# A new stored order, with an accumulating form of the layernorm statistics, in an RWKV attention and Fourier mixing kernel

## The chip, the cores and the metric

The kernel runs on one core of one Trainium2 chip. The metric is the time of one execution on the device, in microseconds (us), the median of several runs. A core has five instruction queues that work side by side: PE (the matrix unit), ACT, DVE, POOL and SP. SP does no arithmetic here; it issues DMA transfers. Each queue takes its instructions strictly in order, and they wait for each other by semaphores.

## The reference

Two stages, for a batch of 4, 8 heads, 768 steps, head size 48. The first is a linear attention with a state of 48 x 48 per head:

```python
for t in range(S):
    cur = np.einsum('bhd,bhe->bhde', u[None] * kt, vt)
    y[:, :, t] = np.einsum('bhd,bhde->bhe', rt, state + cur)
    state = wt[:, :, :, None] * state + np.einsum('bhd,bhe->bhde', kt, vt)
```

Its output, with the heads side by side, is a row of 384 numbers for each of the 768 steps. The second stage mixes these rows:

```python
X = np.fft.fft(np.fft.fft(x, axis=1), axis=2)
u = x + np.real(X)
un = (u - mean(u)) / sqrt(var(u) + 1e-06)          # over the 384
out = u + np.maximum(un @ w_ch1, 0.0) @ w_ch2      # 384 -> 1536 -> 384
```

All inputs and the output are float32.

## The kernel before, in words

**Tiling.** Each batch is cut into 6 chunks of 128 steps, 24 in all; I write (b,c) for chunk c of batch b. A chunk is loaded as four tiles of 128 x 384 (r, k, v, w; L622, issued by SP). Per chunk, `attention` does this:

- ACT takes the logarithm of w (into `lb`), and PE sums it over the steps with triangular masks (L795 for one direction, L818 for the other; the sum can instead be formed by a subtraction on DVE, L832, form "sum_add" against "sum_two").
- ACT takes exponentials of the sums (L822, L848), and DVE or POOL form the decayed rows `rkh` = r·e and k·e (L849, and k·e in a call that the profile shows at L576), the product r·k (L800, shown at L576), r·k·u, its sum `dc` over each head (DVE, L863) and v·dc (`vtd`).
- `rkh` is transposed to `rkt`: by PE with an eviction by DVE or ACT (forms "tr_two", L890, and "tr_one", L902) or, in batch 3, by a DMA that SP issues (form "tr_dma", L880).
- PE forms the 128 x 128 products of a chunk for all heads (`amat`, L913), DVE masks them (L923; or ACT copies them and DVE or POOL masks the copy), PE updates the state (L950) and forms the chunk's output (L975, L978), to which v·dc is added on DVE (L989), or on PE by a float32 matmul with the identity (form "add_pe", L998).

After the 6 chunks of a batch, `mix` does the second stage for 6 blocks of 128 rows. The Fourier transform over steps is a product with cosine and sine tables of the folded rows (`sd`, `xf`; L1054), the one over the 384 is another (L1098) whose result is added to x into `uf`. Then come the statistics of each row: in batch 0 by an addition that also sums (L1115) and a Square on ACT that sums; in batches 1 to 3 by a plain addition (L1128), a `bn_stats` (L1155) and a `bn_aggr` (L1157) on DVE. The row without its mean (`un`) is transposed for three blocks at a time (one half of a batch: by PE, L1173, or by a DMA, L1180), multiplied with W1 (L1205), passed through ReLU into `ht` (ACT L1213 or DVE L1211), multiplied with W2 (L1224), scaled and added to `uf` (L1233) and stored (L1244). The weights come by POOL's DMA queue (L765, L770).

**Order.** The program is first recorded as a list of operations, each with its engines, buffers and a cost. Where an operation can be done in several forms, `choose` records all of them as alternatives. Which alternative is taken, which engine does an operation, and in which order each engine works, stands in the literal `ORDER`: five lists of operation numbers, one per queue, found offline by a planner in the class `_Prog`. `schedule` walks the lists and puts a planned time on every operation; its constants (costs in ns, `xfer` for the length of a transfer, `T_LAT` for the latency of a DMA transpose, `DMA_SW` for a software queue) serve this plan alone. `emit` writes the instructions in the order of the lists, with semaphores derived from buffers. So the lists set the order, and numbers in the lists are positions in the record: every alternative that is added renumbers what stands behind it.

`vec` is the helper that records an operation for DVE or POOL, `evict` one for ACT or DVE:

```python
def vec(n, fn, **kw):
    return op(None, {"pool": p_1(n), "dve": v_1(n)}, fn, port=("dve",), **kw)
```

Thirty-two small matmuls without use (L1291) and 16 at the start (L1257) stand in PE's list to keep its clock up; they are the same in number before and after.

## Time and profile before

| what | value |
|---|---|
| runs shown | 182.51, 183.09, 184.56 us; median 183.09 us |
| the profiled execution: its own time | 181.76 us |
| its span in the trace (first to last instruction) | 179.6 us |
| granted PE clock | 0.999 |
| instructions | 4554 |
| busy: ACT | 127.5 us (71%) |
| busy: POOL | 107.7 us (60%) |
| DMA | 29.28 MB, mean 163 GB/s |

The profile of one execution has a page (busy time by engine, the span in 40 slices with a digit of tenths for each, the chain of work that ended last, and groups of instructions by line) and a trace that can be asked for the same things over shorter stretches. A row of the timeline reads: start in us, length in us, engine, line, operation, output <- inputs with partitions x elements and type, count, and in brackets the idle time before it with what ended it. A row of groups reads: line, engine, operation, output <- inputs, count | busy us, mean ns of one | idle us before, and what ended it. The chain's rows read: start, length, engine, output, line. On one engine instructions are pipelined: one can start before the row of the one before has ended, so the cost of an instruction in a full queue is the distance between two starts.

### The profile page before, as it was taken

Reading aid. Unit: us, or ns where it says so; the run is one execution under the profiler, and the core shown is the slowest. Engines: PE = TensorE matmul, PEld = TensorE weight load, DVE = VectorE, ACT = ScalarE, POOL = GpSimd, SP = SyncE. Lnnn points to the kernel's source line nnn. Section 1 sums busy time; section 2 is a strip of 40 time slices with the busy share of each in tenths; the row PEclk is TensorE's granted clock in tenths of the full one; section 3 lists DMA queues with packets and bytes.
Section 4 is the critical chain, followed back from the end, with each engine's and each line's share of the span. In section 5 each row is a group of like instructions: output and inputs, shape, how many; then the busy total and the mean of one; then the engine's idle time right before and its main releaser. Section 6 shows DMA issues by size and latency. Waiting matters only on the chain.

```text
span 179.6 us, 4554 instructions
## 1 busy us (share of the span) xinstructions
PE 172.1 (96%) x1704; PEld 113.7 (63%) x1704; DVE 159.5 (89%) x378; ACT 127.5 (71%) x306; POOL 107.7 (60%) x134
## 2 busy tenths in 40 slices
PE   4989899999999999999999999999989999999994
PEld 2456556766666667777666666766656766655663
DVE  7899899989999899999999999999999997971643
ACT  2899978679996578799999897989960775062200
POOL 2557969496705888499999964997862140500000
PEclk9999999999999999999999999999999999999999
DMA  6999999999999689999997999989972213034033
GB/s 118 217 210 225 183 206 193 203 216 179 162 205 204 145 173 224 199 211 217 202 239 137 224 182 240 235 155 197 245 71 56 74 47 65 1 60 141 0 131 131
DMA packets 117302, 29.28 MB, mean 163 GB/s; under 512 B 112545, under 2 KB 117282, under 8 KB 117282
## 3 DMA queue, kind: packets, MB, share of 16 engines
q1 hardware_dynamic: 115698, 26.65, 72.3%
q0 software_dynamic: 1584, 2.36, 7.9%
q8 instruction: 13, 0.21, 0.5%
q14 instruction: 7, 0.06, 0.1%
HBM read 23.59 MB, written 4.72 MB: 158 GB/s over the span
## 4 chain that ended last, share of the span: by engine, by line
PE 72%; DVE 13%; ACT 7%; POOL 3%; DMA 3%; issue 1%; POOLq 0%; DVEq 0%; ACTq 0%
PE bank L1205 23%; PE bank L1224 23%; PE bank L1098 4%; PE bank L1054 3%; PE bank L913 3%; DMA rkt<-rkh 3%; PE bank L890 2%; PE bank L795 2%; PE bank L978 2%; DVE bst L1155 2%; PE bank L975 1%; DVE uf L1128 1%; ACT rkt L599 1%; PE bank L950 1%; PE bank L818 1%
## 5 line engine op out<-in xcount | busy, mean ns | idle before, releaser
L1224 PE MATMUL bank<-w,ht 128*128 128x384 bf16 (+2 forms) x300 | 53.1, 320 | 0.0
L1205 PE MATMUL bank<-unt,w 128*128 128x384 bf16 x288 | 52.9, 326 | 0.0
L1213 ACT ACTIVATE ht<-bank 128x384 bf16<-128x384 f32 x70 | 31.0, 496 | 21.1 <-PE bank L1205 20.9
L1224 PEld LDWEIGHTS bank<-w,ht 128*128 128x128 bf16 x300 | 27.8, 98 | 15.6
L1205 PEld LDWEIGHTS bank<-unt,w 128*128 128x128 bf16 x288 | 26.6, 98 | 15.8 <-ACT ht L1213 0.2
L923 DVE TENSOR_TENSOR ah<-bank,msk 128x512 bf16<-128x512 f32 x44 | 28.7, 682 | 0.8 <-PE bank L913 0.6
L576 POOL TENSOR_TENSOR rk<-in_r,in_k 128x384 f32<-128x384 f32 x22 | 21.8, 999 | 1.9 <-issue 1.4
L576 POOL TENSOR_TENSOR rkh<-in_k,e 128x384 bf16<-128x384 f32 x18 | 18.0, 1003 | 6.7 <-ACT e L836 4.9
L576 POOL TENSOR_TENSOR rk<-rk,ub 128x384 f32<-128x384 f32 x20 | 19.8, 998 | 3.3 <-DVE rk L576 2.1
L576 POOL TENSOR_TENSOR vtd<-in_v,dc 128x384 f32<-128x384 f32 x20 | 16.4, 829 | 5.1 <-DVE sd L576 1.8
L599 ACT ACTIVATE rkt<-bank 128x512 bf16<-128x512 bf16 (+1 forms) x23 | 16.3, 713 | 4.3 <-PE bank L902 2.8
L1233 DVE SCALAR_TENSOR_TENSOR osb<-bank,rstd,uf 128x384 f32<-128x384 f32 (+2 forms) x24 | 14.3, 594 | 5.5 <-PE bank L1224 3.5
L1211 DVE TENSOR_SCALAR ht<-bank 128x384 bf16<-128x384 f32 x26 | 13.5, 548 | 5.4 <-PE bank L1205 5.2
L863 DVE TENSOR_REDUCE dc<-rk 128x8 f32<-128x384 f32 x24 | 12.7, 544 | 0.4 <-POOL rk L576 0.4
L848 ACT ACTIVATE bank<-bank 128x384 f32<-128x384 f32 x22 | 10.6, 488 | 3.0 <-PE bank L795 2.7
L590 ACT ACTIVATE lb<-in_w 128x384 bf16<-128x384 f32 x24 | 12.6, 528 | 0.1
L590 ACT ACTIVATE un<-uf,agg 128x384 bf16<-128x384 f32 x19 | 11.2, 618 | 1.5 <-DVE agg L1157 0.9
L849 DVE TENSOR_TENSOR rkh<-bank,in_r 128x384 bf16<-128x384 f32 x22 | 11.9, 547 | 0.2 <-ACT bank L848 0.2
L590 ACT ACTIVATE vb<-in_v 128x384 bf16<-128x384 f32 x22 | 11.5, 530 | 0.4 <-DMA in_v<-in_v_dram 0.3
L822 ACT ACTIVATE e<-bank 128x392 f32<-128x392 f32 (+1 forms) x18 | 8.8, 498 | 3.9 <-PE bank L809 2.5
L978 PE MATMUL bank<-vb,ah 128*128 128x48 bf16 x192 | 11.2, 183 | 0.0
L576 POOL TENSOR_TENSOR xf<-sd 128x384 bf16<-128x384 f32 (+1 forms) x7 | 6.9, 1002 | 6.1 <-DVE xf L576 3.9
(178 smaller groups left out, 365.1 us busy)
## 6 DMA issues: line engine op xcount, KB each, us to landing
in_r<-in_r_dram SPq DMA_DIRECT2D x24, 192.0 KB, 3.9
in_k<-in_k_dram SPq DMA_DIRECT2D x24, 192.0 KB, 3.8
in_w<-in_w_dram SPq DMA_DIRECT2D x24, 192.0 KB, 3.8
in_v<-in_v_dram SPq DMA_DIRECT2D x24, 192.0 KB, 3.8
out_dram<-osb SPq DMA_DIRECT2D x23, 192.0 KB, 2.9
w<-in_moe_w_ch_dram POOLq DMA_DIRECT2D x2, 576.0 KB, 7.9
w<-in_moe_w_ch_dram POOLq DMA_DIRECT2D x1, 1152.0 KB, 10.7
out_dram<-osb SPq DMA_DIRECT2D x1, 128.0 KB, 1.8
```

The costliest lines, as they stand in the source:

```text
L576: return lambda e: e.tensor_tensor(out=o, in0=a, in1=b, op=f)
L590: return lambda e: e.activation(o, a, f, **kw)
L599: {"act": lambda e: e.activation(o(), i(), ACTF.Copy), "dve": lambda e: e.tensor_copy(out=o(), in_=i())}, **kw)
L849: op("dve", v_1(DM), lambda e: e.tensor_tensor(out=rh[:, :, 0:D], in0=ps(tce)[:, 0:DM].rearrange("t (h d) -> t h d", d=D), in1=rt[:, :, :] ...
L863: op("dve", v_1(DM), lambda e: e.tensor_reduce(out=dc[:, :], in_=rku[:, :, :], axis=mybir.AxisListType.X, op=ALU.add), r=[("RK", i2)], w=[ ...
L923: masked[n].append(op("dve", v_1(512), lambda e: e.tensor_tensor(out=ah[:, x:H:2, :], in0=ps(bk)[:, :].rearrange("p (h t) -> p h t", t=128 ...
L978: ins = e.matmul(ps(ty)[:, D * h:D * h + D], ah[:, h, :], vb[:, h, :], start=first and not ype, stop=True, skip_group_check=True)
L1205: ins = e.matmul(ps(t)[:, 0:384], W1[:, m, 256 * (j // 2) + j % 2:256 * (j // 2) + 256:2], unt[:, :, m, :], start=(m == 0), stop=(m == NM ...
L1211: {"dve": lambda e, j=j, t=t, ht=ht: e.tensor_scalar(out=ht[:, j, :], in0=ps(t)[:, 0:384], scalar1=su, scalar2=0.0, op0=ALU.mult, op1=ALU. ...
L1213: "act": lambda e, j=j, t=t, ht=ht: e.activation(ht[:, j, :], ps(t)[:, 0:384], ACTF.Relu, scale=su)},
L1224: ins = e.matmul(ps(t)[:, 0:hi - lo], ht[:, j, 128 * x:128 * x + 128], W2[:, j, lo:hi], start=(j == 0), stop=(j == NJ - 1))
L1233: op("dve", v_1(hi - lo) + 64, lambda e: e.scalar_tensor_tensor(out=o[:, lo:hi], in0=ps(t)[:, 0:hi - lo], scalar=rstd[:, kb:kb + 1], in1=u ...
```

## The change

Four things are changed.

1. `ORDER` is replaced. 1 operation less is on PE (559 to 558), 9 more on ACT (300 to 309), 3 fewer on DVE (372 to 369) and 3 fewer on POOL (130 to 127); SP has 133 in both. Read against the record, the new lists differ in these places above all:
   - *First loads:* before, SP issued r1, k1, w1, w0, u, r0, k0 first; after, w0, k1, u, r1, w1, k0, r0, w2 (the digit is the chunk of batch 0).
   - *Batch 0, products:* r·k of chunks (0,1), (0,2) and (0,3) and k·e of (0,0) go from POOL to DVE; r·k·u of (0,1), v·dc of (0,0) and k·e of (0,2) and (0,4) go from DVE to POOL.
   - *Batch 0, others:* chunk (0,1) takes its output addition on DVE (L989) instead of PE (L998; two other chunks keep that form); two casts of the transform in mix 0 go from DVE to ACT; evictions of transposes are dealt differently between ACT and DVE, with "tr_one" and "tr_two" swapped in six chunks. The decay sums of (1,0) take "sum_two" in place of "sum_add", those of (3,4) the reverse.
   - *Statistics:* blocks 0, 1 and 2 of mix 2 and block 2 of mix 3 take the new form `add_sum`.
   - *Late, on SP:* before, the order was: last loads of (3,5), load v of (3,4), outputs (1,5), (1,3), (1,4), DMA transposes of (3,5) and (3,4), transpose of the second half of mix 2. After, it is: load v of (3,4), transposes of (3,4) and (3,5), load v of (3,5), outputs (1,3), (1,5), transpose of the second half of mix 2, output (1,4). On PE, `amat` of these two chunks stands earlier by two groups of W2 matmuls and one state update. On POOL, k·e of (3,5) stands earlier.
2. Constants of the plan: a load counts 998 ns instead of 985, the stretch that a transfer of the software queue (the weights) takes up in the plan begins 200 ns earlier, the DMA transposes of (3,4) and (3,5) count 200 ns more and that of the second half of mix 2 200 ns more.
3. New buffers `MS` and `MCO`, with two small fills on DVE.
4. A new alternative `add_sum` for the statistics of batches 1 to 3. The bn_stats, bn_aggr and the operation that subtracts the mean are moved from behind the choice into each alternative.

The diff without the lists:

```diff
+    MS = [sb("ms%d" % i, [NC, 3], FP32) for i in range(2)]
+    MCO = sb("mco", [2], FP32)
...
                 a = max(sw_t, s + self.DMA_SW)
                 sw_t = a + o.xfer
+                a -= 200
...
-               w=[("in", n, i)], sem="in_%s%d" % (n, i), xfer=985)
+               w=[("in", n, i)], sem="in_%s%d" % (n, i), xfer=998)
...
+        op("dve", 40, fill(MCO[:, 0:1], 1.0 / DM), w=["MCO0"])
+        op("dve", 40, fill(MCO[:, 1:2], float(DM) ** -1.5), r=["MCO0"], w=["MCO"])
...
-               ... xfer=T_XFER, dma=(T_LAT[0], T_LAT[1] + 500))
+               ... xfer=T_XFER, dma=(T_LAT[0], T_LAT[1] + (700 if (b, c) >= (3, 4) else 500)))
...
+                def normed(mean, dep, kb=kb, un=un, iu=iu):
+                    op(None, {"act": a_sb(DM) + 95, "dve": v_2(DM) + 60},
+                       {"act": act(un, uf[:, kb, :], ACTF.Identity, scale=-1.0, bias=mean),
+                        "dve": ts(un, uf[:, kb, :], mean, -1.0, ALU.subtract, ALU.mult)}, port=("dve",),
+                       r=[("UF", i, kb), dep], w=[("UN", iu, kb % 3)])
+
+                def stats(kb=kb, bs=BST[n % 4], n=n):
+                    op("dve", v_1(DM), lambda e: e.bn_stats(bs[:, :], uf[:, kb, :]), ...)
+                    op("dve", 89, lambda e: e.bn_aggr(agg[:, kb, :], bs[:, :]), ...)
+                    normed(agg[:, kb, 0:1], ("AGG", i, kb))
...
+                def add_sum(kb=kb, t=t):
+                    whole()
+                    ms = MS[i]
+                    op("dve", v_1(DM) + 60, lambda e: e.scalar_tensor_tensor(
+                        out=uf[:, kb, :], in0=ps(t)[:, 0:DM], scalar=1.0, in1=xb[:, kb, 0:DM], op0=ALU.mult, op1=ALU.add,
+                        accum_out=ms[:, kb, 2:3]), r=[t, ("X", i, kb)], w=[("UF", i, kb), ("SUM", i, kb)])
+                    op("dve", 64, lambda e: e.tensor_tensor(
+                        out=ms[:, kb, 0:2], in0=ms[:, kb, 2:3].to_broadcast([128, 2]), in1=MCO[:, :], op=ALU.mult),
+                       r=[("SUM", i, kb), "MCO"], w=[("MS", i, kb)])
+                    normed(ms[:, kb, 0:1], ("MS", i, kb))
+                    op("act", a_sb(DM) + 190, act(xf[:, kb, 63:447], uf[:, kb, :], ACTF.Square, scale=-float(DM) ** -0.5,
+                                                  bias=ms[:, kb, 1:2], accum_out=agg[:, kb, 1:2]),
+                       r=[("UF", i, kb), ("MS", i, kb)], w=[("AGG", i, kb)] + [(z, i, kb) for z in ("XFe", "XFo", "XFn")])
-                g.choose(("u", b, kb), add_bank, add_row, add_parts)
+                g.choose(("u", b, kb), add_bank, add_row, add_parts, add_sum)
...
-                       dma=(T_LAT[0], T_LAT[1] + (550 if b < 3 else 150)))
+                       dma=(T_LAT[0], T_LAT[1] + (750 if (b, hf) == (2, 1) else 550 if b < 3 else 150)))
```

With `add_sum`, the addition leaves the sum of the row beside it, a multiplication of two elements per row makes the mean and a shift from it, and ACT forms the variance by a Square with a sum.

More of the change, by code (lines that the diff above doesn't have):

```diff
@@ L881, in tr_dma @@
                                                            in_=RKH[i4][:, :, :, :].rearrange("t x h d -> t (x h d)")),
[L882 removed]
+               r=[("RH", i4), ("KH", i4)], w=[("RTB", i4), ("KTB", i4)], sem="rkt%d" % i4, xfer=T_XFER, dma=(T_LAT[0], T_LAT[1] + (700 if (b, c) >= (3, 4) else 500)))
         def tr_two():
@@ L1125, in mix @@
             else:
+                def normed(mean, dep, kb=kb, un=un, iu=iu):
[4 more added lines that the diff above has]
+                def stats(kb=kb, bs=BST[n % 4], n=n):
+                    op("dve", v_1(DM), lambda e: e.bn_stats(bs[:, :], uf[:, kb, :]),
+                       r=[("UF", i, kb)], w=[("BST", n % 4)])
+                    op("dve", 89, lambda e: e.bn_aggr(agg[:, kb, :], bs[:, :]),
+                       r=[("BST", n % 4)], w=[("AGG", i, kb)])
+                    normed(agg[:, kb, 0:1], ("AGG", i, kb))
                 def add_bank(kb=kb, t=t):
```

13 lines of the change are left out of this document (3 added, 10 removed), and 139 rows, old and new, of the table ORDER.

## The prediction

> **What bounds the kernel now.** I read the page first: the span, the busy shares, the forty slices and the shares of the chain that ended last.
>
> ```profile
> span 179.6 us, 4554 instructions
> PE 172.1 (96%) x1704; PEld 113.7 (63%) x1704; DVE 159.5 (89%) x378; ACT 127.5 (71%) x306; POOL 107.7 (60%) x134
> ...
> PE   4989899999999999999999999999989999999994
> ...
> DVE  7899899989999899999999999999999997971643
> ...
> PEclk9999999999999999999999999999999999999999
> ...
> PE 72%; DVE 13%; ACT 7%; POOL 3%; DMA 3%; issue 1%; POOLq 0%; DVEq 0%; ACTq 0%
> ```
>
> PE is busy for 96% of the span at its full granted clock, so only about 7.5 us (179.6 - 172.1) of the span can come back without removing matmuls. The second view is the table by stage. Its columns are the stretch, its length, then busy time and count for PE, PEld, DVE, ACT and POOL, then clock, DMA share and GB/s.
>
> ```profile
> 0.00:10.00 10.00, 7.51 (x31) 3.44 (x31) 8.23 (x39) 6.21 (x9) 3.71 (x14) 1.00 0.87 172
> 10.00:20.00 10.00, 8.90 (x129) 6.21 (x129) 9.62 (x21) 9.60 (x22) 7.73 (x9) 1.00 1.05 205
> 20.00:30.00 10.00, 9.34 (x119) 5.87 (x118) 9.60 (x20) 8.99 (x22) 8.42 (x12) 1.00 1.02 202
> 30.00:40.00 10.00, 9.80 (x110) 7.09 (x108) 9.10 (x29) 6.71 (x16) 7.54 (x9) 1.00 1.14 207
> 110.00:120.00 10.00, 10.00 (x108) 7.07 (x106) 9.71 (x22) 8.52 (x21) 9.84 (x11) 1.00 1.00 212
> 120.00:130.00 10.00, 10.00 (x98) 6.42 (x98) 10.00 (x24) 9.10 (x22) 8.39 (x10) 1.00 0.98 215
> 130.00:140.00 10.00, 9.49 (x95) 6.03 (x94) 9.59 (x22) 3.75 (x12) 4.27 (x5) 1.00 0.52 76
> ```
>
> PE has holes in two places only: 4.45 us before 40 us (2.49 + 1.10 + 0.66 + 0.20), where batch 0 runs alone and DVE is the fullest engine from 10 us on, and 0.51 us at 130 to 140. At 110 to 130 PE has none, though DVE is full as well. The third view, the chain of waits with the timeline, shows what ends each hole.
>
> ```profile
> 18.99 0.96 POOL rk L576
> 20.02 1.01 POOL rk L576
> ...
> 23.60 0.47 DVE rkh L849
> ...
> 99.49 0.65 PE bank L1224 x4
> ```
>
> ```profile
> 21.05 0.55 DVE L863 TENSOR_REDUCE dc<-rk 128x8 f32<-128x384 f32 x1 [0.36 <-POOL rk L576]
> ```
>
> ```profile
> 124.37 0.47 DVE bst L1155
> 124.84 0.46 DVE uf L1128
> ...
> 126.22 0.09 DVE agg L1157
> ...
> 128.14 0.47 DVE rkh L849
> ...
> 128.63 4.57 DMA rkt<-rkh
> 133.19 0.04 issue
> 133.24 0.40 PE bank L913 x8
> ```
>
> ```profile
> 130.75 0.33 PE L950 MATMUL bank<-vb,rkh 128*128 128x96 bf16 x4
> ...
> 132.33 0.40 PE L913 MATMUL bank<-rkt 48*128 48x128 bf16 x8
> 133.24 0.40 PE L913 MATMUL bank<-rkt 48*128 48x128 bf16 x8 [0.51 <-DMA rkt<-rkh]
> ```
>
> Early, the chain alternates between ACT, POOL products of about 1 us and DVE instructions of about 0.47 us start to start. Late, it goes along DVE until 128.63 us, then along the transpose of the last chunk by DMA, and the PE waits 0.51 us for that transpose.
>
> **The change part by part.** The sum is made against the profiled execution, 181.76 us (span 179.6 us and 2.16 us around it); the median of the runs shown is 183.09 us, 1.33 us above, and I carry the same difference over to it. Counts of instructions come from the two stored lists, decoded against the program.
>
> *Early stretch.* Up to the first addition of batch 0's mix (L1115), DVE has 93 instructions instead of 95. Leaving it: four products, a row product, an accumulating sum, two casts of the transform, a fold, an eviction and small fills, 4.79 us by their rows. Arriving: three products r*k and one k*e from POOL, the addition for chunk (0,1), an eviction for (0,3), three transposes' evictions, a fold, a mirror and a fill, 5.10 us. DVE thus carries 0.31 us more; POOL ahead of the first weight load has 0.34 us less and ACT ahead of the first normalised row 0.5 us less, by the same count. Against that, waits of DVE for POOL's products, such as the 0.36 us at 21.05, should fall: a product r*k on DVE takes half the time.
>
> ```profile
> L576 POOL TENSOR_TENSOR rk<-in_r,in_k 128x384 f32<-128x384 f32 x22 | 21.8, 999 | 1.9 <-issue 1.4 <-DVE rkh L576 0.5
> ...
> L576 DVE TENSOR_TENSOR rkh<-in_k,e 128x384 bf16<-128x384 f32 x6 | 3.6, 601 | 0.1
> ...
> L576 DVE TENSOR_TENSOR rk<-in_r,in_k 128x384 f32<-128x384 f32 x2 | 1.1, 548 | 0.0
> ```
>
> Bounds: DVE has 1.68 us idle from 10 to 40 us (0.38 + 0.40 + 0.90); if 1.3 us of it goes and the 0.31 us come, this gives -1.0 us; if none goes and an exclusion between the two engines (below) adds half a microsecond, +0.8 us. I take -0.3 us, nearer to the row of 0.36 us than to either end. The new order of the first loads (w, k and u ahead of r) only permutes equal transfers; it is inside these bounds.
>
> *One float addition fewer on PE.* Chunk (0,1) no longer adds v*dc by a pair of half passes in float32 (L998).
>
> ```profile
> 13.78 0.91 PE L998 MATMUL bank<-vtd,ht 128*128 128x384 f32 x2
> 14.53 0.39 PE L890 MATMUL bank<-idw,rkh 128*128 128x128 bf16 x4
> ```
>
> From the start of that pair to what follows are 0.75 us of PE work; a second term matmul of chunk (1,0) is added and one of (3,4) removed, each near a third of a microsecond, so they cancel. The pair lies where PE had 1.10 us of holes in ten, so its removal widens a hole: 0, with -0.7 us as the other end (all of it on the path). What covers it is the DVE queue; if DVE gets early, the 0.7 us count.
>
> *Statistics in the accumulating form*, for blocks 0 to 2 of mix 2 and block 2 of mix 3. Gone on DVE for each: addition 0.46, statistics 0.47, aggregation 0.09 = 1.02 us. New: the addition with its sum and a multiplication of two elements.
>
> ```profile
> 37.47 0.56 DVE L1115 SCALAR_TENSOR_TENSOR uf<-bank,x 128x384 f32<-128x384 f32 x1 [0.43 <-PE bank L1098]
> 37.96 0.08 DVE L1115 DVE_READ_ACCUMULATOR uf<-bank,x 128x1 f32 x1
> 37.96 0.56 DVE L1115 SCALAR_TENSOR_TENSOR uf<-bank,x 128x384 f32<-128x384 f32 x1
> ```
>
> ```profile
> L590 ACT ACTIVATE xf<-uf,agg 128x384 bf16<-128x384 f32 x6 | 3.7, 624 | 0.0
> ...
> L590 ACT ACTIVATION_READ_ACCUMULATOR xf<-uf,agg 128x1 f32 x6 | 1.2, 207 | 0.0
> ```
>
> The addition costs 0.49 us start to start, the small one I set like the aggregation, 0.09 us: 0.58 us, so -0.44 us a block and -1.3 us for the three in mix 2, where DVE is on the chain (114 to 128 us). But PE is at 10.00 of 10 us there: DVE's gain shortens nothing that PE waits for, except the way to the last transposes, counted next. I take 0. Bounds: -0.5 us and, should ACT become late, +0.5 us. ACT's new Squares cost at most 0.83 us each (0.624 + 0.207), 2.5 us for three, against 2.38 us of idle ACT at 110 to 130 us: nearly all of this cover is used, and what would be late next are the W1 activations (L1213) that PE's W2 groups read. That multiplication waits for the addition on the same queue, and every later DVE instruction stands behind it, but no other engine ends that wait.
>
> *Late transposes.* On SP, the transposes of (3,4) and (3,5) were issued after three outputs.
>
> ```profile
> 124.53 1.87 SPq L1244 DMA_DIRECT2D out_dram<-osb  x3
> 127.19 2.68 SPq L880 DMA_TRANSPOSE rkt<-rkh  x2
> ```
>
> Now they stand ahead of those outputs, with one load (v of (3,5)) and the outputs behind them; whatever waits on SP for those products holds that load and the outputs back. The products' DVE work ahead of the later transpose is 1.6 us less by my count. PE wants it earlier, too: two groups of W2 matmuls (2 x 0.65) and one state update (0.33) stood ahead of those matmuls and now follow, about 1.6 us. Both shifts are equal; the 1.87 us of outputs no longer in front help where SP, not DVE, was the last. Bounds: the 0.51 us hole closes (-0.5), or PE's wish comes 1.6 us earlier with the landings as before (+1.6). I take -0.2 us, near the closed hole, because the chain reaches this transpose straight from DVE's product (L849 at 128.14, DMA at 128.63 us), so DVE's shorter queue moves it. The planner's constants, among them 985 to 998 for a load and the 200 of margin, move no instruction by themselves: 0.
>
> Sum: -0.3 + 0 + 0 - 0.2 = -0.5 us; 181.76 becomes 181.3 us in the profiled execution, and 183.09 becomes 182.6 us.
>
> **The rivals.** *Late stall (slower).* The two transposes land when they did, near 132 and 133 us, while PE reaches them 1.6 us earlier; full DVE and POOL queues (10.00 and 8.39 of 10 us) speak for it, since POOL's product for (3,5) now stands some 3 us earlier in its queue and would wait for its load of k. Against it stand DVE's shorter queue and the outputs out of the way. PE then waits about 0.5 + 1.6 us before L913 of (3,4) or (3,5); with the early gain that is 183.09 - 0.3 + 1.6 = 184.4 us, and half a microsecond to 1.5 us more if the held POOL queue makes the products themselves late. I put it at 184.9 us. It decides from a landing of the second transpose later than about 131.6 us (133.2 - 1.6).
>
> *DVE and POOL in each other's way (slower).* The product row of DVE with two operands in SBUF shows 601 ns on average for k*e, against 548 for r*k: some of them ran beside POOL and were stretched. Three more such products enter DVE in the densest stretch. If each holds DVE for one POOL product (999 ns), half of the time on the path, that is 3 x 0.999 / 2 = 1.5 us, and 0.2 us of the added work: 184.8 us. Against it: POOL has 0.34 us less to do, and the products taken away from DVE were of the same kind, four against four. [...]
>
> *The early stretch gives all (faster).* The early DVE gain reaches its bound (-1.0), PE's removed pair then counts (-0.7) and the hole at 133 us closes (-0.5): 183.09 - 2.2 = 180.9 us. For it: PE's holes lie there, 4.45 us of them. Against it: DVE carries 0.31 us more in that stretch.
>
> *It does not do what it says.* The accumulating form is worth nothing, as DVE's time is covered by PE; that is inside the forecast, and with no gain elsewhere the time is 183.1 us.
>
> **How the numbers follow.** Forecast and its last variant together 0.54, at 182.6 us, own range 181.4 to 183.9; late stall 0.17 at 184.9; engines in each other's way 0.13 at 184.8; all of the early stretch 0.16 at 180.9. A measurement of this kernel can tell about 1% from no change, which is 181.26 to 184.92 us. Faster by more: most of the last rival, 0.13, and 0.03 of the forecast's tail, 0.16. Slower by more: half of each slow rival, 0.085 + 0.065, and 0.03 of the tail, 0.18. Within 1%: 0.66. The range from 180.7 to 185.0 us leaves out about 0.07 below and 0.13 above.
>
> **What would show it.** Early: the first L1205 matmul comes 0.3 us earlier than in the profile before, and the reduction L863 waits less for POOL. Statistics: 14 rows of L1155 in place of 18, 10 Squares, a shorter DVE part of the chain from 114 to 128 us, and PE still full there. Late: the wait at L913 is shorter than 0.51 us and the rkt transposes start near 125.5 us instead of 127.19. I am wrong if PE has a hole over 1 us near 130 us (late stall), if L1205 starts later (exclusion), if ACT's L1213 makes PE wait at 115 to 130 us, or if the early holes shrink by more than a microsecond.

## The result, and the profile after

| | before | changed |
|---|---|---|
| median of 17 runs each | 182.84 us (181.74 to 187.15) | 184.80 us (183.04 to 185.43) |
| profiled execution, its own time | 181.76 us | 184.72 us |
| span in the trace | 179.6 us | 182.5 us |
| granted PE clock, mean over the span | 0.999 | 0.981 |

The ratio is 1.0107, with a 95% interval from 1.0083 to 1.0131: the change makes the kernel slower by about 1.1%, some 2.0 us. I had forecast 0.5 us faster. Measured again on another chip (e9 below), the ratio was 1.0085 [1.005, 1.012]. Executions more than 1.5% above the fastest of their kernel are left out of the ratios and of the means by clock below, but not of the medians.

The page of the changed kernel first. Helpers and the new code shift its lines: the W1 matmul is L1232, the W2 matmul L1251, `amat` L919, the PE transposes L896, the float addition L1004, the idle matmuls L1318.

```profile
span 182.5 us, 4564 instructions
...
PE 174.6 (96%) x1702; PEld 115.0 (63%) x1702; DVE 156.6 (86%) x379; ACT 133.0 (73%) x319; POOL 105.3 (58%) x131
...
PEclk9995699999999999999999999999999999999999
...
PE 81%; DVE 8%; ACT 5%; DMA 2%; SPq 1%; issue 1%; POOL 0%; DVEq 0%; POOLq 0%
```

PE is busy for 2.5 us longer (174.6 against 172.1) with two matmuls fewer, and DVE 2.9 us shorter. The one row that looks different in kind is that of the clock: in the fourth and fifth slice (about 14 to 23 us) it is down to 5 and 6 tenths. In the profile before it was 9 in all 40. So PE did not get more work; the same work took longer. The table by stage says where.

```profile
0.00:10.00 10.00, 7.64 (x28) 3.55 (x29) 6.62 (x34) 5.55 (x8) 2.93 (x13) 1.00 0.83 161
10.00:20.00 10.00, 8.72 (x80) 5.45 (x79) 8.11 (x19) 7.96 (x19) 6.46 (x8) 0.73 1.06 208
20.00:30.00 10.00, 9.34 (x141) 6.70 (x139) 9.75 (x21) 8.23 (x16) 8.34 (x12) 0.93 1.03 200
...
120.00:130.00 10.00, 9.65 (x118) 6.29 (x117) 9.40 (x21) 9.38 (x24) 9.29 (x11) 1.00 1.02 177
130.00:140.00 10.00, 9.25 (x92) 5.83 (x92) 9.73 (x24) 5.88 (x14) 8.11 (x9) 1.00 0.79 147
```

From 10 to 20 us PE gets through 80 matmuls at a mean clock of 0.73, where it did 129 at 1.00 before. DVE and ACT, which were at 9.62 and 9.60 there, fall to 8.11 and 7.96: the waits for PE that the profile lists in this stretch are 1.5 us on DVE and 2.1 us on ACT, where they were 0.3 us on each. And from 120 to 140 us PE has 1.10 us of holes (0.35 + 0.75), where it had 0.51.

How much lies in each part is read from the first and the last W1 matmul, in the view of one line's instructions (durations min/median/max, first and last start). Before, after, and, for later, the experiment e7:

```profile
L1205 PE MATMUL bank<-unt,w x288: 322/326/337, 41.4 to 170.2; 128*128 128x384 bf16 x144
```

```profile
L1232 PE MATMUL bank<-unt,w x288: 323/326/338, 43.2 to 173.8; 128*128 128x384 bf16 x144
```

```profile
L1230 PE MATMUL bank<-unt,w x288: 322/326/338, 41.4 to 171.8; 128*128 128x384 bf16 x144
```

Batch 0 ends 1.8 us later (43.2 against 41.4). From there to the last W1 it takes 130.6 us instead of 128.8, and from the last W1 to the end 8.7 instead of 9.4: together 1.1 us. The profiled executions thus differ by 2.9 us, 1.8 early and 1.1 late. The medians differ by 2.0 us only, since the profiled execution of before was 1.1 us under its median.

Stretches of two microseconds around the dip, after:

```profile
12.00:14.00 2.00, 1.21 (x10) 0.69 (x9) 1.95 (x5) 1.53 (x4) 0.07 (x1) 1.00 1.11 221
14.00:16.00 2.00, 1.87 (x19) 1.14 (x19) 1.41 (x3) 1.46 (x4) 2.00 (x4) 0.63 1.03 202
16.00:18.00 2.00, 1.99 (x15) 1.15 (x16) 2.00 (x6) 1.80 (x5) 1.29 (x2) 0.50 1.11 220
18.00:20.00 2.00, 2.00 (x12) 1.19 (x11) 1.09 (x4) 1.54 (x5) 1.14 (x2) 0.50 1.01 197
20.00:22.00 2.00, 1.58 (x34) 1.50 (x32) 2.00 (x6) 1.83 (x4) 1.40 (x3) 0.66 1.05 205
```

And the first of these before:

```profile
12.00:14.00 2.00, 1.91 (x35) 1.50 (x32) 1.89 (x5) 2.00 (x6) 0.77 (x2) 1.00 1.03 198
```

The clock is 0.50, half, through two whole stretches, and the mixed ones give its ends: (1 - 0.63) / 0.5 = 0.74 of the second stretch and (1 - 0.66) / 0.5 = 0.68 of the last, so half clock from about 14.5 to 21.4 us. The trace keeps records of the clock, and they say the same: full clock from 7.70 us for 6.83 us, half for 6.83 us, then full to the end. In the stretch ahead of the fall PE is thin: busy for 1.21 of 2 us with 10 matmuls, where it was busy for 1.91 with 35. PE's timeline shows with what.

```profile
12.82 0.40 PE L896 MATMUL bank<-idw,rkh 128*128 128x128 bf16 x4 [0.79 <-DVE rkh L580]
13.15 0.26 PE L755 MATMUL bank<-ss,unt 64*128 64x193 bf16 x1
13.34 0.44 PE L755 MATMUL bank<-cs,idw 1*128 1x193 bf16 x2
...
16.71 1.63 PE L1004 MATMUL bank<-vtd,ht 128*128 128x384 f32 x2
...
22.39 0.40 PE L919 MATMUL bank<-rkt 48*128 48x128 bf16 x8
```

A wait of 0.79 us for the product k·e, then matmuls of the transform's tables with only 64 and 1 of the 128 rows in use (they stood at 9.09 to 10.28 us before). Behind the fall, the float pair takes 1.63 us, where a pair took 0.91 and 0.86.

Not all of the 1.8 us of batch 0 comes from this fall. The first triangular sum starts 1.0 us later already: the full clock itself came at 7.70 us instead of 5.23, and the 16 starting matmuls took 5.30 us instead of 4.22. It starts as late in e2 (below), which has the early lists of before, the full clock from 7.81 us and no fall, and there the first W1 comes at 42.1 us. The first sums of before, after and e2, then the W1 matmuls of e2:

```profile
8.35 0.34 PE L795 MATMUL bank<-lb,msk 128*128 128x384 bf16 x1 [0.22 <-ACT lb L590]
```

```profile
9.32 0.34 PE L801 MATMUL bank<-lb,msk 128*128 128x384 bf16 x1
```

```profile
9.33 0.34 PE L797 MATMUL bank<-lb,msk 128*128 128x384 bf16 x1
```

```profile
L1228 PE MATMUL bank<-unt,w x288: 322/326/338, 42.1 to 172.7; 128*128 128x384 bf16 x144
```

So I estimate that in this pair of profiles about 0.7 us (42.1 - 41.4) goes with the late first full clock, which also occurs with the lists of before, and about 1.1 us (43.2 - 42.1) with the fall.

The statistics and the late transposes are shown with their experiments below.

### The profile page after: what moved, and what is told of

Its sections match the earlier page's. It is cut to its first block, busy times and chain, and to the rows that moved or that the text cites. A ratio compares the mean times of both kernels' runs of the same rounds, so it can differ in the third digit from the quotient of the medians.

```text
span 182.5 us, 4564 instructions
## 1 busy us (share of the span) xinstructions
PE 174.6 (96%) x1702; PEld 115.0 (63%) x1702; DVE 156.6 (86%) x379; ACT 133.0 (73%) x319; POOL 105.3 (58%) x131
## 4 chain that ended last, share of the span: by engine, by line
PE 81%; DVE 8%; ACT 5%; DMA 2%; SPq 1%; issue 1%; POOL 0%; DVEq 0%; POOLq 0%
PE bank L1232 23%; PE bank L1251 23%; PE bank L919 4%; PE bank L1104 4%; PE bank L1060 3%; PE bank L1318 3%; PE bank L896 3%; PE bank L1284 3%; DMA in_r<-in_r_dram 2%; PE bank L984 2%; PE bank L801 2%; PE bank L908 2%; PE bank L981 2%; PE bank L956 1%; DVE rkh L855 1%; PE bank L1065 1%
## 5 line engine op out<-in xcount | busy, mean ns | idle before, releaser
L1251 PE MATMUL bank<-w,ht 128*128 128x384 bf16 (+2 forms) x300 | 53.0, 319 | 0.0
L1232 PE MATMUL bank<-unt,w 128*128 128x384 bf16 x288 | 52.4, 326 | 0.0
L1240 ACT ACTIVATE ht<-bank 128x384 bf16<-128x384 f32 x74 | 32.6, 494 | 11.8 <-PE bank L1232 11.7
L1251 PEld LDWEIGHTS bank<-w,ht 128*128 128x128 bf16 x300 | 27.6, 98 | 15.3
L1232 PEld LDWEIGHTS bank<-unt,w 128*128 128x128 bf16 x288 | 26.7, 98 | 16.1 <-DMA unt<-un 0.4
L929 DVE TENSOR_TENSOR ah<-bank,msk 128x512 bf16<-128x512 f32 x43 | 28.0, 680 | 0.9 <-PE bank L919 0.8
L1260 DVE SCALAR_TENSOR_TENSOR osb<-bank,rstd,uf 128x384 f32<-128x384 f32 (+2 forms) x22 | 12.8, 594 | 10.2 <-DMA out_dram<-osb 5.2
L580 POOL TENSOR_TENSOR vtd<-in_v,dc 128x384 f32<-128x384 f32 x23 | 19.0, 829 | 2.4 <-DVE dc L869 2.4
L580 POOL TENSOR_TENSOR rk<-in_r,in_k 128x384 f32<-128x384 f32 x17 | 16.9, 1001 | 5.3 <-DVE rkh L580 5.2
L603 ACT ACTIVATE rkt<-bank 128x512 bf16<-128x512 bf16 (+1 forms) x19 | 12.7, 688 | 2.4 <-PE bank L896 1.2
L580 POOL TENSOR_TENSOR xf<-sd 128x384 bf16<-128x384 f32 (+1 forms) x8 | 8.0, 1004 | 10.3 <-DVE xf L580 8.0
L1238 DVE TENSOR_SCALAR ht<-bank 128x384 bf16<-128x384 f32 x22 | 11.8, 550 | 1.5 <-PE bank L1232 1.4
L995 DVE TENSOR_TENSOR x<-bank,vtd 128x384 f32<-128x384 f32 x22 | 12.1, 551 | 0.8 <-PE bank L984 0.8
L896 PE MATMUL bank<-idw,rkh 128*128 128x128 bf16 x96 | 10.0, 230 | 1.6 <-DVE rkh L580 0.8
```

The costliest lines, as they stand in the source:

```text
L580: return lambda e: e.tensor_tensor(out=o, in0=a, in1=b, op=f)
L603: {"act": lambda e: e.activation(o(), i(), ACTF.Copy), "dve": lambda e: e.tensor_copy(out=o(), in_=i())}, **kw)
L896: ins = e.transpose(psb(t)[:, 128 * h:128 * h + 128], rows[:, 128 * h:128 * h + 128], IDB[:, :])
L929: masked[n].append(op("dve", v_1(512), lambda e: e.tensor_tensor(out=ah[:, x:H:2, :], in0=ps(bk)[:, :].rearrange("p (h t) -> p h t", t=128 ...
L1232: ins = e.matmul(ps(t)[:, 0:384], W1[:, m, 256 * (j // 2) + j % 2:256 * (j // 2) + 256:2], unt[:, :, m, :], start=(m == 0), stop=(m == NM ...
L1240: "act": lambda e, j=j, t=t, ht=ht: e.activation(ht[:, j, :], ps(t)[:, 0:384], ACTF.Relu, scale=su)},
```

## The experiments

Theories at the start: *clock* (PE thin after the start loses its full clock, and batch 0 ends late), *order* (the new order of batch 0 makes chunk (0,2), whose `amat` comes at 22.39 instead of 18.50 us, late by itself), *late* (the new order on SP and PE at 120 to 135 us), and *form* (the accumulating statistics cost time). An idle matmul in the diffs is one more of the matmuls without use (L1318), written W; PE's list is shown by what stands beside it. The idle matmuls change no result.

**e1: five idle matmuls in the wait at 12 us.**

```diff
-NW = 32
+NW = 37
...
-  PE: ... transposes at 11.64, transposes at 12.82 ...
+  PE: ... transposes at 11.64, W W W W W, transposes at 12.82 ...
```

> The changed kernel with 5 more matmuls without use on PE, ahead of the transposes of k*e of chunk (0,0), where PE waited 0.79 us at 12.82 us; nothing else is altered. Theory clock (PE is thin at 11 to 14.5 us, so the granted clock is 0.5 for 6.8 us from 14.5 us and the matmuls of batch 0 take twice as long): the granted clock rises from 0.981 to 0.99 or 1.0 and the time falls from 184.8 to 183.0 to 183.9 us. Theory order (the new early queues themselves delay chunk (0,2), by POOL and DVE): the clock may rise, but the time stays at 184.4 to 185.2 us. Theory late (the holes at L919 near 122 and 134 us): no change, 184.6 to 185.0 us.

183.70 us, 1.0077 [1.0048, 1.0106]. Three of six executions at clock 0.991, three at 1.0, with the same mean time (183.77 and 183.63). In the profiled one the fall came at 20.1 us and lasted 3.4 us. One wait filled moves the fall and shortens it; it doesn't remove it.

**e2: the early order of before with all else of the change.** Lists of before up to the first block of mix 0, the changed ones behind, constants as before.

> A splice: everything that stands before about 38 us of the plan in the order, forms and engines of the kernel before, with its constants, and the rest in the order of the changed kernel. Theory early (clock or order): the first W1 matmul is back near 41.4 us instead of 43.2, and the time at 182.4 to 183.4 us. Theory late: the holes near 122 and 134 us remain, 0.8 us more than before, so 183.4 to 184.0 us with the early loss gone; 184.4 us or more would mean that the early stretch is not the cause.

182.42 us, 1.0021 [0.9997, 1.0045], the clock at 0.999 or 1.0 in all 12. Most of the loss thus lies in the early order; what is left for late and form together is 0.4 us by the ratio (0.0021 x 182.27), 0.8 us by its upper end.

**e3: the change with the statistics of before.**

```diff
-  mix 2 blocks 0, 1, 2 and mix 3 block 2: add_sum
+  the same blocks: add_bank (addition, bn_stats, bn_aggr)
```

> The changed kernel with the four blocks of statistics in the plain form (addition, bn_stats, bn_aggr) again at the same places of the queues, and the four Squares taken out of ACT. Forecast's reason (PE covers it): 184.4 to 185.2 us, no difference to the changed kernel. If DVE's time at 115 to 135 us is on the path, the last transposes come 1 us later and the time is 185.3 to 186.0 us. If the Squares made ACT late, it is below 184.4 us.

184.60 us, 1.0124 [1.0098, 1.015]; clock 0.981 in all six. The form doesn't carry the bulk of the loss.

**e4: the order of before, started cold.**

```diff
-PSUM_STATE, NE = 1, 16
+PSUM_STATE, NE = 1, 4
```

> The kernel before with 4 instead of 16 matmuls without use at the start, all else as it was: PE is too thin there for the full clock. Theory clock: the granted clock in the first 20 us is 0.5 for one or more windows, and the time rises from 182.8 to 184.0 to 186 us, by at least 0.15 us for each microsecond at half clock. If batch 0 is bound by the other engines and not by PE, the clock falls and the time stays within 0.5 us of 182.8 us.

183.16 us, 1.0065 [1.0042, 1.0087], and the first W1 at 43.2 us, as in the changed kernel. Here the trace has no record of the clock at all and its column reads 1.00, but the matmuls tell it: the same form (128 x 384, one at a time) is long until 13 us (0.50 to 0.53 us; it is 0.53 in the changed kernel at 18.13 us, where the granted clock is 0.50) and short from 17 us on (0.32 to 0.34).

```profile
8.96 0.53 PE L795 MATMUL bank<-lb,msk 128*128 128x384 bf16 x1
...
17.42 0.34 PE L795 MATMUL bank<-lb,msk 128*128 128x384 bf16 x1
```

So the early lists of before lose 1.8 us at their first W1, and 1.2 us by the ratio, when PE is slow for about the first 13 to 17 us. Matmuls as slow as at half clock, in batch 0 alone, are enough for a loss of the measured size.

**e5: chunk (0,2) forward.** Its decay sum, exponential and decayed rows earlier in four lists.

```diff
-  PE: ... float addition for (0,0), decay sum of (0,2) ...
+  PE: ... decay sum of (0,2), float addition for (0,0) ...
   (ACT: an exponential, DVE: a fill and r·e, POOL: k·e of (0,2) moved likewise)
```

> The changed kernel with chunk (0,2) taken forward in four queues, each step to where its inputs are there: on PE its cumulative sum goes ahead of the float addition for (0,0), on ACT its exponential ahead of three table evictions and a cast, on DVE its product with r (and the fill of that buffer) ahead of the second mask of (0,1), and on POOL its product with k ahead of its v*dc. No operation is added. Theory order (the matmuls of (0,2) came at 22.39 us instead of 18.50, held by those queues): L919 of (0,2) comes 2 us or more earlier, the first W1 matmul 0.8 us or more earlier than 43.2, and the time is 182.8 to 183.8 us. Theory clock alone: the granted clock is still near 0.981, and the time stays at 184.3 to 185.0 us.

183.94 us, 1.0122 [1.0086, 1.0157]. `amat` of (0,2) came at 20.44 us, 2 us earlier than in the changed kernel's profile, but this profile held the full clock, and where the changed lists hold it without the edit (e14) it comes at 20.68 us. The edit itself moved it by 0.2 us, so e5 says little about *order*. Within the kernel the clock splits the executions: 182.87, 183.34 and 183.48 us at 1.0, and 184.40, 184.53 and 184.80 at 0.98: 1.35 us on the mean.

**e6: e1 and e5 together.**

> Both: the 5 matmuls without use at 12.8 us and chunk (0,2) taken forward. If clock and order each cost a part (0.6 us and 1.2 us of the 1.9 lost), the time is 182.2 to 183.2 us, the granted clock 0.99 or more, and the first W1 matmul at 41.2 to 42.2 us. If they are the same loss told twice, it is no faster than the better of the two alone (183.4 us or more).

183.18 us, 1.0091 [1.0063, 1.0119]; first W1 at 42.1 us. By the ratio no more than e1 alone (1.0077).

**e7: sixteen idle matmuls in five waits from 12 to 21 us.**

```diff
-NW = 32
+NW = 48
...
+  PE: W x5 ahead of the transposes at 12.82, W x2, W x2, W x3 and W x4 in four waits behind
```

> The changed kernel with 16 matmuls without use on PE at five waits between 12 and 21 us (5, 2, 2, 3 and 4 of 0.16 us each), so that PE is thin nowhere there. Theory clock: the clock is 1.0 in all executions, and the time 182.6 to 183.4 us. Theory order: the clock is 1.0 and the time still 183.4 to 184.2 us, since the waits on DVE, POOL and ACT remain (what was measured with 5 of them, 183.7 us, is then all that the clock is worth).

182.32 us, 1.0039 [1.0012, 1.0066]; clock 0.999 or 1.0 in all 12 executions. The first stage and the same stretch of two microseconds:

```profile
10.00:20.00 10.00, 9.62 (x107) 5.80 (x108) 9.25 (x22) 8.56 (x20) 7.00 (x11) 1.00 1.01 197
12.00:14.00 2.00, 2.00 (x21) 1.12 (x21) 1.55 (x4) 1.53 (x4) 0.78 (x1) 1.00 1.13 224
```

Without other changes the clock holds, and the first W1 comes at 41.4 us, where it came before the change (row above), although `amat` of (0,2) is at 20.76 us still. This settles *clock* against *order*. In the profile the whole 1.8 us of batch 0 are back, with a full clock that also came earlier (6.27 us, against 7.70 in the changed kernel's). By the ratios, which average over the starts, matmuls that compute nothing bring back 0.5 to 0.7% (1.0039 against 1.0085 in e9 and 1.0107), or 0.8 to 1.2 us. What remains, 0.4%, is late, form or the idle matmuls themselves (e10): from the first to the last W1 130.4 us, against 128.8 before.

**e8: a load ahead of the transpose of `un` on SP.**

```diff
-  SP: transpose of un (mix 2), load r, load k, load r, load v ...
+  SP: load r, transpose of un (mix 2), load k, load r, load v ...
```

> The changed kernel with the load of r for (3,4) on SP ahead of the transpose of mix 2's first half, which waits for its rows: three loads stood behind that wait, among them r of (3,5) for the last product ahead of the last transposes. Theory late: the last transposes land 0.6 us earlier, the hole at L919 near 134 us shrinks from 0.8 to 0.3 us, and the time is 184.2 to 184.6 us. If that transpose is itself on the path of the W1 matmuls at 126 us, a hole appears there and the time is 184.8 to 185.8 us.

184.87 us, 1.0168 [1.014, 1.0197]. At clock 0.981 its three executions average 184.92 us, those of the changed kernel on the same chip (e9, four) 184.51: nothing gained. Changed kernel, the chain of waits, then the timelines of DVE and PE around 120 to 135 us, then the transposes of this stretch with their time to landing:

```profile
122.97 0.76 SPq L1207
...
125.02 4.24 DMA in_r<-in_r_dram
...
129.36 0.56 DVE rkh L855
```

```profile
129.36 0.56 DVE L855 TENSOR_TENSOR rkh<-bank,in_r 128x384 bf16<-128x384 f32 x1 [0.59 <-DMA in_r<-in_r_dram]
```

```profile
122.52 0.40 PE L919 MATMUL bank<-rkt 48*128 48x128 bf16 x8 [0.34 <-DMA rkt<-rkh]
...
134.48 0.40 PE L919 MATMUL bank<-rkt 48*128 48x128 bf16 x8 [0.75 <-DVE agg L1141]
```

```profile
L886 SPq DMA_TRANSPOSE rkt<-rkh x2: 1233/1272/1310, 127.9 to 130.0; - x2
...
DMA to landing us min/median/max: 3.2/3.8/4.4
```

PE of e8:

```profile
126.62 6.01 PE L1229 MATMUL bank<-unt,w 128*128 128x384 bf16 x36 [0.54 <-DMA unt<-un]
134.71 0.40 PE L916 MATMUL bank<-rkt 48*128 48x128 bf16 x8 [0.45 <-DVE ht L1235]
```

In the changed kernel SP is held by the transpose of `un` until 123.73 us (122.97 + 0.76). The load of r for the last chunk stands behind it and two more loads, is issued at 125.02 and lands at 129.26; DVE waits 0.59 us for it and makes the product from 129.36 to 129.92; SP issues its transpose at 130.0, and 4.4 us later, at 134.4, PE goes on. (Its row puts the 0.75 us down to `agg`, on which `amat` does not depend; the landing of the transpose fits to a tenth of a microsecond.) Moving a load ahead takes DVE's wait away, but makes the transpose of `un` late for W1: a new hole of 0.54 us, through which DVE is late again for the same product. Neither passes the other for free.

**e9: the changed kernel again,** beside e10 to e12.

> The changed kernel itself, as the base of the others on this chip: 1.0107 of the kernel before, granted clock 0.981 in most executions, and the executions at clock 1.0 about 1 us faster than those at 0.981 (theory clock) or no faster (theory order).

184.41 us, 1.0085 [1.005, 1.012]. By clock: 0.981 in four (mean 184.51), 0.991 in two (183.40), 1.0 in three (182.35, 182.58 and 182.79; mean 182.57). The 28 executions of before beside it were all at 1.0, mean 182.03. At full clock the changed kernel is thus 0.5 us slower than before, with the fall 2.5 us. The mean clock doesn't show when the full clock first came, so the step between the two, 1.9 us, may hold a late start too.

**e10: the order of before with ten idle matmuls,** the control for e7.

```diff
-NW = 32
+NW = 42
...
+  PE: W x5 in one wait of batch 0 and five more in four others
```

> A control: the kernel before with 10 matmuls without use at its waits on PE between 10.8 and 18.5 us (5, 1, 2, 1 and 1). Its clock is 1.0 without them. Theory clock: they give nothing here, 0.997 to 1.003 of the kernel before. If matmuls without use help in some other way than by the clock, it is faster than before by 0.3% or more.

182.62 us, 1.0046 [1.002, 1.0072]: slower. The idle matmuls were no gain here, where the clock didn't fall (0.999 or 1.0 in all 12 executions).

**e11: the narrow table matmuls into the wait.**

```diff
-  PE: ... transposes at 11.64, transposes at 12.82, tables (64 and 1 rows) ...
+  PE: ... transposes at 11.64, tables (64 and 1 rows), transposes at 12.82 ...
```

> The changed kernel with one group of narrow matmuls of the tables (1 or 64 rows of the array, 13.15 to 14.28 us) moved on PE ahead of the transposes of k*e of (0,0), into the wait of 0.79 us; no operation added. The first amat then stands 0.4 us earlier. Theory clock, as the busy time of PE goes: the wait is filled, so the clock stays at 1.0 and the time is 183.0 to 183.9 us. If these narrow matmuls count as little as idleness for the clock, it still falls to 0.98 or 0.99, and the time is 184.2 to 185.0 us.

183.62 us, 1.0102 [1.0077, 1.0127]; three executions at 1.0 (mean 183.35), one at 0.991, two at 0.981 (184.15). The fall is not removed; whether it is rarer, six executions can't tell.

**e12: the accumulating statistics alone, in the order of before.** The four blocks take `add_sum`, with the new buffers and fills; nothing else moves.

> The accumulating statistics alone: the kernel before, in its own order and with its constants, with the four blocks in the accumulating form and the four Squares right behind the rows without mean on ACT. Forecast's reason (PE covers DVE's gain): 0.997 to 1.004 of before. If DVE's 1.3 us count, 0.992 to 0.997. If the Squares (0.83 us each at most) delay ACT's activations, over 1.004.

182.75 us, 1.0039 [1.0012, 1.0066]: no gain, rather a loss. The small multiplication shows why the gain was small at best. Changed kernel, DVE and POOL in mix 2, then DVE in mix 3:

```profile
119.03 0.80 DVE L1182 TENSOR_TENSOR ms<-ms,mco 128x2 f32<-128x2 f32 x2
119.75 0.54 DVE L869 TENSOR_REDUCE dc<-rk 128x8 f32<-128x384 f32 x1
120.21 0.50 DVE L1182 TENSOR_TENSOR ms<-ms,mco 128x2 f32<-128x2 f32 x1
120.64 1.13 DVE L1260 SCALAR_TENSOR_TENSOR osb<-bank,rstd,uf 128x384 f32<-128x384 f32 x2
```

```profile
118.73 1.97 POOL L580 TENSOR_TENSOR rk<-in_r,in_k 128x384 f32<-128x384 f32 x2
```

```profile
150.74 0.15 DVE L1182 TENSOR_TENSOR ms<-ms,mco 128x2 f32<-128x2 f32 x1
150.85 0.36 DVE L580 TENSOR_TENSOR uf<-uf,xf 128x191 f32<-128x191 f32 x1
```

In mix 2 two of them take 0.72 us start to start (119.75 - 119.03), one alone 0.43 us: about four times the 0.09 us that I set. In mix 3 it takes 0.11 us (150.85 - 150.74). The difference is POOL: it is idle at 150.7, and in mix 2 it works on two products of 1 us each, from 118.73 to 120.70. The last multiplication starts at 120.21 in the second product and ends at 120.71 with it; of the first two, one takes 0.72 us and so ends at about 119.75, where POOL's first product ends. The two long k·e behind the prediction's 601 ns, of 0.73 us from 12.03 and 0.68 us from 23.98 us in the kernel before, began while POOL worked too (11.34 to 12.34 and 22.56 to 24.25 us). With the addition at 0.49 us a block of mix 2 costs 0.85 to 0.92 us against 1.02 before, a gain of 0.10 to 0.17 us in place of 0.44.

**e13: the order of before with 12 starting matmuls.**

```diff
-PSUM_STATE, NE = 1, 16
+PSUM_STATE, NE = 1, 12
```

> The kernel before with 12 instead of 16 matmuls without use at the start. The full clock came at 5.4 us in one profile and at 7.5 to 7.7 us in others, and in the late case the 16 take 5.3 us and push the first sums from 8.35 to 9.3 us. Theory start (this shift reaches the end): 0.994 to 0.999 of before, with a smaller spread. If too few remain for the full clock, it is 1.003 or more, as with 4.

182.44 us, 1.0029 [1.0, 1.0058]. The clock fell in six of 12 executions: mean 182.1 us at 0.999 and 1.0, 183.0 at 0.991 (five), 183.72 at 0.981 (one). The order of before was not far from falling either.

**e14: the new lists with the old constants** (985 for 998, no 200 of margin, 500 and 550 for the transposes).

> The changed kernel in its new order, with the old constants of the plan (985, no margin, 500 and 550). Five operations get other waits by it. Prediction's step (constants move nothing): 1.0085 to 1.0107 of before, as the changed kernel, with most executions at a clock of 0.981. If a wait matters, more than 0.3% away from that.

184.07 us, 1.0106 [1.0072, 1.014], with the clock below 1.0 in five of six. The constants carry nothing, as forecast. The one at full clock is the profiled one, and shows the new lists, without idle matmuls, where the clock does not fall:

```profile
L1231 PE MATMUL bank<-unt,w x288: 322/326/338, 41.3 to 172.4; 128*128 128x384 bf16 x144
```

```profile
10.00:20.00 10.00, 7.16 (x94) 4.76 (x95) 9.26 (x22) 8.67 (x20) 6.97 (x11) 1.00 1.02 204
```

PE has even larger holes here, 2.84 us in ten against 1.28 at the lower clock, and yet the first W1 comes at 41.3 us, as before the change. By themselves these holes cost nothing here; the 1.9 us go with the clock, in this pair of profiles its earlier start (5.20 against 7.70 us) and the missing fall together.

**e15: e11 with eleven idle matmuls** (2, 2, 3 and 4 in the four later waits of e7), **and e16: the same with 12 starting matmuls.**

> The changed kernel with both means against the thin stretch: the narrow matmuls in the wait at 12 us, and 11 matmuls without use at four later waits. Theory clock: clock 1.0 in all executions, first W1 matmul near 41.2 us, 1.001 to 1.004 of before; what is left over 1.000 is the late part (about 1 us of holes at 110 to 135 us against 0.6). If narrow matmuls count as idle, part of the executions is at 0.98 to 0.99 and the ratio 1.005 to 1.009.

> The same with 12 instead of 16 matmuls without use at the start. Theory start: 0.3 to 0.6 us faster than with 16, so 0.997 to 1.002 of before. If the clock then falls in the first 10 us, slower than with 16.

e15: 183.72 us, 1.0092 [1.0057, 1.0128]; clock 0.981 in four of seven (184.22), 1.0 in three (182.96). e16: 182.54 us, 1.0033 [1.0014, 1.0052]; 0.999 or 1.0 in all 12. Their tables from 10 to 20 us, e15 first:

```profile
10.00:20.00 10.00, 9.00 (x71) 5.41 (x72) 8.03 (x19) 7.28 (x17) 5.82 (x8) 0.66 1.05 207
```

```profile
10.00:20.00 10.00, 9.14 (x112) 5.71 (x113) 9.46 (x23) 8.67 (x20) 7.17 (x11) 1.00 0.98 193
```

The orders are the same; the four starting matmuls fewer keep the clock here, and lost it in e13. PE is as busy by its row (9.00 and 9.14 us) and does 71 or 112 matmuls in it: so with a granted clock of 0.66 in one and 1.00 in the other, busy time is no measure of work. No version was faster than before.

## Why the prediction was wrong

**The step that failed** is the early stretch, "I take -0.3 us", with its bounds of -1.0 to +0.8 us. Its sum was near: at full clock the new lists bring the first W1 at 41.3 us (e14), 0.1 earlier instead of 0.3; and "its removal widens a hole: 0", said of PE's float pair, holds there too. But the step took the granted clock of 1.00 in the table of before as given. With the new lists it fell in 9 of 12 executions (e9), and with sixteen idle matmuls in five of PE's waits in none of 12 (e7). In the changed kernel's profile the first W1 comes 1.8 us later, outside the bounds, about 1.1 us of it by the fall; by the ratios 0.8 to 1.2 us of the 2.0 us come back when the clock is held (e7). The bounds had no term for it, as I counted what DVE, POOL and ACT gain and lose, and not what the new list of PE puts where: the narrow table matmuls and the wait for k·e fell together at 12 to 14 us. The sign "L1205 starts later" did come, but I had tied it to the exclusion between DVE and POOL.

How often and how much: at 0.98 or 0.99 in 14 of the 17 runs of the comparison and in 9 of 12 in e9; never below 0.999 in the 92 executions of before beside e1 to e16. Between executions of one kernel at 0.98 and at 1.0 lie 0.8 us (e11), 1.0 (the 17 runs), 1.3 (e15), 1.35 (e5) and 1.9 (e9). What late and form leave at full clock is 0.4 us (e2), 0.5 (e9), 0.7 (e7), 1.0 (the three of the 17 runs at 1.0, mean 183.85) or 1.4 (the one of e14, 183.33 against 181.95). The two together make the 2.0 us of the comparison; their shares are known no better than this, but the step with the clock is the larger in e9, where both are measured side by side (1.9 and 0.5).

**When it falls.** From the clock's records in the profiled executions, in us from the span's start:

| kernel | full clock from | half clock |
|---|---|---|
| before | 5.23 | none ahead of 179.31 |
| changed | 7.70 | 14.52 to 21.35 |
| e9, changed again | 7.02 | 13.85 to 20.68 |
| e3 | 6.80 | 13.63 to 20.46 |
| e8 | 7.70 | 14.53 to 21.35 |
| e5, e14, e11 | 5.10, 5.20, 5.40 | none |
| e1 | 6.42 | 20.08 to 23.49 |
| e13 | 4.91 | 11.74 to 15.15 |
| e15 | 6.41 | 13.24 to 20.06 |
| e7, e16, e2 | 6.27, 7.21, 7.81 | none |
| e12, e10 (lists of before) | 7.41, 7.99 | none |
| e4, e6 | no record | no record |

In these profiles the full clock came between 4.91 and 7.99 us, and where it fell, this was 6.83 us after (13.65 in e1), for 3.41 or 6.83 us. In the changed order it fell in the profiles with a late start (6.4 to 7.7), but for e7 and e16 (6.27 and 7.21, with idle matmuls), and not in those with an early one (5.1 to 5.4); with the early order of before (e2, e12, e10) it held at 7.41 to 7.99 too. Executions of the changed order at 0.98 and at 1.0 thus differ in their start as well as in the fall. In the 3.4 us ahead of the fall in the changed kernel's profile PE was busy for 2.61 us:

```profile
11.10:14.50 3.40, 2.61 (x35) 1.76 (x33) 3.16 (x8) 2.56 (x7) 1.44 (x2) 1.00 1.10 213
```

What stays open is the measure that decides; no run shows it. Busy time alone isn't it: in e5 the clock held behind 2.34 us of work in a stretch of this length. The same stretch, from 3.4 to 6.8 us after the full clock came, in e15 (2.60 us), which fell, and in e16 (2.71) and e5 (2.34), which held:

```profile
9.80:13.20 3.40, 2.60 (x30) 1.68 (x27) 3.35 (x9) 2.39 (x6) 1.52 (x2) 1.00 1.09 212
```

```profile
10.60:14.00 3.40, 2.71 (x37) 1.86 (x33) 3.15 (x8) 2.67 (x6) 1.43 (x2) 1.00 1.04 206
```

```profile
8.50:11.90 3.40, 2.34 (x30) 1.51 (x29) 2.95 (x9) 3.03 (x8) 1.95 (x2) 1.00 1.07 212
```

Whether narrow matmuls count for less was not separated (e11 was inconclusive), nor what part the removed float pair has, since it was not put back alone; nor why 12 starting matmuls kept the clock in e16 and lost it in e13.

**Late transposes:** forecast -0.2 us, measured about +0.6 us of holes at `amat`: 0.34 and 0.75 in place of 0.51. "Both shifts are equal" was the mistake. The last of these transposes was issued at 128.6 before and 130.0 after,

```profile
L880 SPq DMA_TRANSPOSE rkt<-rkh x6: 1231/1241/1587, 103.3 to 128.6; - x6
```

and set against the first W1 that is 87.2 and 86.8 us: 0.4 us earlier, not 1.6, while PE came to it 1.6 us earlier by my count. What held it was the load of r behind SP's wait for `un`, a wait that the prediction did not follow. This is the *late stall* by mechanism: its landing came after the point from which it decides (131.6, with batch 0's delay of 1.8 us 133.4, measured 134.4), at about a third of its price. By itself it stays within 1%. The rest of the 1.1 us late was not assigned. The profiles, one of each, say only that the late lists and the form each bring holes without the other: PE's holes from 110 to 140 us are 0.51 us before, 0.99 with the late lists and the plain form (e3), 0.99 with the form in the lists of before (e12), and 1.10 with both; from the first to the last W1 it is 128.8, 130.7, 130.2 and 130.6 us.

**Statistics:** taken as 0 with bounds of 0.5 us on both sides. On DVE the gain in mix 2 is 0.1 to 0.2 us a block, not 0.44: the small multiplication, set like the aggregation at 0.09 us, took 0.36 (the mean of two) to 0.43 us while POOL worked on its products and 0.11 us with POOL idle (rows at e12). In the order of before the form costs 0.7 us (e12, 0.2 to 1.2 by its interval); in the changed order, at clock 0.981, the kernel is 184.59 us without it (e3) and 184.72 with it (the 17 runs and e9). So it gains nothing, and how much of the rest at full clock it carries, beside the late part, stays open. **Constants:** 0, shown by e14.

**DVE and POOL in each other's way:** not seen on the moved products. The product k·e on DVE takes less on average than before (601 ns):

```profile
L580 DVE TENSOR_TENSOR rkh<-in_k,e 128x384 bf16<-128x384 f32 x6 | 3.3, 552 | 0.1
```

It is seen elsewhere: at the small multiplication (e12), and once in e8, where a product on DVE that began 0.09 us behind one on POOL took 1.34 us instead of 0.52 (the changed kernel's at 131.43 us, with POOL idle).

```profile
131.31 1.34 DVE L577 TENSOR_TENSOR rk<-rk,ub 128x384 f32<-128x384 f32 x1
```

```profile
131.22 1.01 POOL L577 TENSOR_TENSOR osb<-osb,uf 128x384 f32<-128x384 f32 x1
```

The rival's time, 184.8 us, is the one measured, but by luck: its price of 1.5 us was for the early products, and the cause lies in the clock.

**The early stretch gives all:** not seen. Where the clock holds, the first W1 comes at 41.1 to 41.4 us (e7, e11, e14, e16; 41.8 in e5) against 41.4 before: the new order of batch 0 gains 0.3 us at most.

## What to carry to other kernels

A granted clock of 1.00 in the profile before is not a constant: in the new order it fell in 9 of 12 executions (e9), and with idle matmuls in PE's waits it held in all 12 (e7). Where a change thins PE out in the first 20 us, give the loss of the clock a rival of its own; here the step between executions of one kernel with and without it was 0.8 to 1.9 us. Compare the clock of each execution before comparing times, and read in each profile when the full clock first came, too: the mean clock doesn't show it (1.0 in e2, with the full clock from 7.81 us), and by my estimate from e2 (42.1 - 41.4) it alone moved the first W1 by some 0.7 us. Where the clock is the suspect, an edit that holds it without changing any result (e7, with its control e10) separates it from the order. Where two queues' shifts are said to cancel, work out each from the queue that issues it, with what it waits for ahead.

## What the runs showed that I had not expected

- Idle matmuls that compute nothing gain about 0.5% where they hold the clock (e7 against e9: 1.0039 and 1.0085) and cost 0.5% where it holds anyway (e10: 1.0046).
- The clock's column reads 1.00 ahead of its first record, even where the matmuls are as slow as at half clock: in e4 a 128 x 384 matmul took 0.53 us at 8.96 us and 0.34 us at 17.42 us, in the changed kernel 0.53 us at 18.13 us, at a granted 0.50.
- A multiplication of two elements per row on DVE takes 0.11 us with POOL idle, and 0.72 us for two or 0.43 us for one while POOL works on a product of its own: the last one ended at 120.71 us, POOL's product at 120.70.
